# Down projection of a GEGLU feed-forward: seven block products for eight in the correction terms of seven of twelve pairs

## The chip, the cores and the metric

The kernel runs on one core of a Trainium2 chip. The metric is the device time of one execution in microseconds (us). Its engines are named as in the profile: PE (TensorE, matrix products), DVE (VectorE), ACT (ScalarE), POOL (GpSimd) and SP (which here only issues DMAs). Each engine works through its own list of instructions in order; semaphores hold an instruction back until what it needs from another engine is done.

## The reference

One transformer layer on 2048 tokens of width D = 640, in float32: attention with a sliding window of 256, then the feed-forward with F = 1536. Only the last matrix product is touched by the change.

```python
x = A_x
h = x + _A_ref(_layernorm(x, axis=-1), A_wqkv, A_wo)
h2 = h + _B_ref(_layernorm(h, axis=-1), B_w_gate, B_w_up, B_w_down)
# _B_ref(x, w_gate, w_up, w_down):
#   (_gelu(x @ w_gate) * (x @ w_up)) @ w_down
```

## The kernel before

**Numbers as pairs.** Float32 operands are split into a high and a low half in float16 (names ending in h and l). A float32 product is then three float16 products: high times high, and the two corrections high times low and low times high.

**Tiling of the feed-forward.** The tokens are cut into four chunks `c` of 512 (four blocks `b` of 128), the width F into three weight groups `fg` of 512 (four tiles `ft` of 128). `ORDER` lists the twelve pairs (c, fg): (0,0), (1,0), (0,1), (0,2), (1,1), (1,2), (2,0), (2,1), (2,2), (3,0), (3,1), (3,2). The first three are done by `gate_up`; the last nine by four calls of `quad` each, one for each `ft`, 36 quads in all, which I number 0 to 35. A quad makes gate and up projections with a scheme of seven block products for eight: its block results come to the PSUM tiles tp, ra, pv and rb (PE `MATMUL tp<-...` and so on), and `quad_out` combines them: ACT copies tp to SBUF, POOL adds the two halves, DVE runs eight operations (`rs<-pv`, two `gel<-ra`, `rs<-pv`, `rs<-rb`, `gel<-rs,ffk,gel`, `al<-gel,ah`; in the trace the tile rr or gelt is the SBUF copy of tp), ACT the gelu and the cast `ah<-gel`. The result is the activation of the pair as `ah` and `al`.

**The down projection.** `down(c, fg)` multiplies `ah`, `al` by the down weights of the group (`dh`, `dl`; in the trace w10h and w10l for group 0, w11 and w12 for groups 1 and 2). It makes eight output tiles (four blocks by two halves of 320 columns), each of 4 x 3 matmuls into a PSUM bank of the pool mm, which has two banks. `down_out` empties each bank with one DVE operation, `ht<-mm,ffk,ht`, which adds it to the float32 accumulator `ht` of the block. `down` of a pair does not run by itself: it is a generator, and `quad` calls `fill` at its end, which takes two tiles from it. So the eight tiles of a pair run in the four quads of the next pair, two after each quad, and only the last pair's `down` stands alone at the end.

**Who sets the order.** A planner (`Clock`, `Engine`, `Lane` and the loop at the end) runs at build time: it keeps a modelled time for each engine and lets the next operation of each generator be issued when its operands are modelled as ready. PE's own sequence in the feed-forward is fixed by the code (`dense_lane`); what DVE, ACT, POOL and SP do between is interleaved by the planner. Side lanes on DVE and POOL share the time of the quads: `norm_lane` and `token_sums` (normalise and pre-sum the next chunks, tiles wsl, ts, wst) and `weight_sums` (pre-sum gate and up weights, tile ws; kept in DRAM as `wsums` and loaded again by SP for pairs whose group has come up before).

Of the kernel before, what the change touches and what calls it, by code (L numbers as in the profile page):

```python
# [11 lines left out]
F32 = mybir.dt.float32  # L12
F16 = mybir.dt.float16
# [9 lines left out]
P = 128  # L23
NB = S // P
# [18 lines left out]
QE = -23  # L43
VE = -20
ME = 15
UE = -41
TE = 10


def _pow2(e):  # L50
    return float(2.0 ** e)
# [202 lines left out]
def block_kernel(ctx: ExitStack, tc: tile.TileContext, x, wqkv, wo, wg, wu, wd, out):  # L254
# [27 lines left out]
    def done(name):  # L282
        opened[name] -= 1
# [35 lines left out]
    def pe(*reads, slots=(), when=None):  # L319
        return ("tensor",), need(*reads, slots=slots, when=when)  # L320
# [23 lines left out]
    ones = const.tile([P, P], F32, name="ones")  # L344
    nc.vector.memset(ones, 1.0)


    NS = 16
# [114 lines left out]
    for g in range(FG):  # L463
        W["g", g] = Weight(wg[g], [KC, 512], C_G + g, GE)
        W["u", g] = Weight(wu[g], [KC, 512], C_U + g, GE)
        W["d", g] = Weight(wd[g], [FT, D], C_D + g)


    def layernorm(xt, lane, hi, lo, dst=None, when=None, xn=None, e=XE, tp="tp",
# [108 lines left out]
    def ff_scales_down(fg):  # L578
        ds_ = C_D + fg
        nc.vector.tensor_scalar(ffk[:, fg, 2:3], ffk[:, fg, 3:4], pw[:, ds_:ds_ + 1],  # L580
                                _pow2(-GE - XE - UE - GE - WE), op0=ALU.mult, op1=ALU.mult)


    wqp = ExitStack()
# [605 lines left out]
    def quad(c, fg, ft, fill):  # L1190
        fs = slice(ft * P, (ft + 1) * P)
        (gh, gl), (uh, ul) = (tuple(t[:, :, fs] for t in W[k, fg].hl) for k in "gu")
        hh, hl = hT[c]
        h1, h2 = hh[:, :, :CW], hh[:, :, CW:]
        l1, l2 = hl[:, :, :CW], hl[:, :, CW:]
        yield pe(slots=["tp"], when=lambda: c in TS and (c, fg, ft) in WS)
        t, s = TS[c], WS.pop((c, fg, ft))
        part = []
        tasks.append(quad_out(c, fg, ft, part))
        xs = bank("tp")  # L1200
        span(xs[:, CW:], gl, h1)
# [9 lines left out]
        span(gs[:, CW:], s[:, 3], l2, start=False)  # L1211
        yield pe(s[:, 2], t[:, 2], slots=["pv"])
        xs = bank("pv")
        span(xs[:, CW:], s[:, 2], t[:, 2])
        yield pe(s[:, 0], t[:, 0])
        span(xs[:, :CW], s[:, 0], t[:, 0])
        part.extend((xs, gs))
        yield pe(slots=["rb"])
        us = bank("rb")
        span(us, uh, hh, stop=False)  # L1220
        yield pe(t[:, 3])
        span(us[:, :CW], uh, t[:, 3], start=False)
        part.append(us)
        pos["quads"] += 1
        yield from fill()

    def quad_out(c, fg, ft, part):
        pool = ffpools[ORDER.index((c, fg)) % 2]
        ah, al = ga[c, fg]
        ra, rb = sums["r", ft % 2], sums["s"]  # L1230
        r2, r1 = ra[:, 0], ra[:, 1]
        r12, r21, r22 = (rb[:, k] for k in range(3))
# [12 lines left out]
        nc.vector.tensor_tensor(rb[:, :2], xs.rearrange("p (a n) -> p a n", a=2),  # L1245
                                r2.unsqueeze(1).to_broadcast([P, 2, CW]), op=ALU.add)
# [8 lines left out]
        nc.vector.tensor_tensor(r22, xs[:, :CW], r21, op=ALU.add)  # L1255
# [5 lines left out]
        nc.vector.tensor_tensor(flat(rb[:, 1:3]), part[3], flat(rb[:, 1:3]), op=ALU.add)  # L1261
        done("rb")
        yield on("vector", gel, rb)
        nc.vector.scalar_tensor_tensor(gel, flat(rb[:, 1:3]), ffk[:, fg, 1:2], gel, op0=ALU.mult,
                                       op1=ALU.mult)
        opened["s"] -= 1
        yield on("scalar", gel)
        nc.scalar.copy(ah[:, ft, :], gel)
        yield on("vector", ah[:, ft, :])
        nc.vector.tensor_tensor(al[:, ft, :], gel, ah[:, ft, :], op=ALU.subtract)  # L1270
        opened["gel"] -= 1
        pos["act", c, fg] += 1

    def down(c, fg):
        w = W["d", fg]
        yield pe(when=lambda: w.ready and w.down and pos["act", c, fg] == FT and c in hts)
        dh, dl = w.hl
        ah, al = ga.pop((c, fg))
        for b in range(CB):
            bs = slice(b * P, (b + 1) * P)  # L1280
            for nh in range(2):
                cs = slice(nh * 320, nh * 320 + 320)
                ps = yield from products(FT, lambda ft: parts((ah[:, ft, bs], al[:, ft, bs]),
                                                              (dh[:, ft, cs], dl[:, ft, cs])))
                tasks.append(down_out(c, fg, b, nh, ps))
                yield

    def down_out(c, fg, b, nh, ps):
        acc = hts[c][b]
        cs = slice(nh * 320, nh * 320 + 320)  # L1290
        yield on("vector", ps)
        nc.vector.scalar_tensor_tensor(acc[:, cs], ps, ffk[:, fg, 2:3], acc[:, cs], op0=ALU.mult,
                                       op1=ALU.add)
        done("mm")
        pos["down", c, b] += 1
        j = c * CB + b
        if pos["down", c, b] == 2 * FG:
# [3 lines left out]
        if j == NB - 1 and pos["down", c, b] > 2 * FG - 2:  # L1301
            nc.sync.dma_start(out[j * P:(j + 1) * P, cs], acc[:, cs])

    chunk = Counter()

    def load_h(c, pool, bufs):
        hts[c] = []
        for b in range(CB):
            j = c * CB + b
            ht = nc.tile(pool, [P, D], F32, "ht", bufs)  # L1310
            nc.sync.dma_start(ht, h_dram[j * P:(j + 1) * P, :])
            hts[c].append(ht)

    def chunk_lane(c):
        yield ("sync",), need(when=lambda: c == 0 or (ffpools[1] if c == 1 else
                                                      chunk["out", c - 2] == CB), eng="sync")
        load_h(c, ffpools[c % 2], CB)

    lnbuf = []

# [214 lines left out]
    def feed_forward():  # L1535
        quads = [(c, fg, ft) for c, fg in ORDER[PLAIN:] for ft in range(FT)]

        def sums_lane():
# [9 lines left out]
        sums["s"] = nc.tile(ffp, [P, 3, CW], F32, "rs")  # L1548
        prev = None
        for c, fg in ORDER[1:PLAIN]:  # L1550
            yield from gate_up(c, fg)
            if prev:
                yield from down(*prev)
            prev = (c, fg)
        for c, fg in ORDER[PLAIN:]:
            groups = down(*prev)

            def fill():
                for _ in range(2):
                    for y in groups:  # L1560
                        if y is None:
                            break
                        yield y

            pool = ffpools[ORDER.index((c, fg)) % 2]
            ga[c, fg] = tuple(nc.tile(pool, [P, FT, CB * P], F16, n) for n in ("ah", "al"))
            for ft in range(FT):
                yield from quad(c, fg, ft, fill)
            pos["gu", c] += 1
            prev = (c, fg)  # L1570
        yield from down(*prev)

    class Lane:
# [143 lines left out]
```

## Time and profile before

| what | value |
|---|---|
| time, median of three runs | 1014.95 us (1013.34 to 1016.89) |
| the profiled execution's own time | 1015.33 us |
| its span in the trace | 1013.6 us |
| PE / DVE / ACT / POOL busy | 98% / 74% / 44% / 31% of the span |
| the 36 quads | about 661 us to 994 us of the span, 9.24 us each |
| the last `down`, alone | 994 us to the end |

The trace gives, for each instruction, its start and length. Lengths of neighbouring instructions on one engine overlap by some tens of ns, since an instruction is begun before the one ahead of it has fully ended; what an instruction adds in a dense stretch is therefore the distance from its start to the next start. PE shows this most: matmuls follow each other much faster than one of them lasts.

### The profile page before, as it was taken

The numbers are of one execution on the slowest core, as the hardware profiler recorded it, in microseconds if no ns is written. First come the engines' busy times: TensorE is split into PE (matmuls) and PEld (weight loads), VectorE is DVE, ScalarE is ACT, GpSimd is POOL, SyncE is SP. The second block draws the span as 40 slices with busy tenths as digits, with TensorE's granted clock in tenths as the row PEclk, the third lists the DMA queues.
The fourth block names the chain that finished last, engine by engine and source line by source line (L and its number), as shares of the span: only waits on it lengthen the run. The fifth ranks groups of instructions, "written<-read, shape, count | busy, mean of one in ns | idle before, by whom it ended". The sixth has DMA issues, their size and how long they took to land.

```text
span 1013.6 us, 30516 instructions
## 1 busy us (share of the span) xinstructions
PE 996.3 (98%) x12798; PEld 696.4 (69%) x12798; DVE 754.7 (74%) x2212; ACT 442.5 (44%) x711; POOL 315.0 (31%) x504
## 2 busy tenths in 40 slices
PE   8999999999999999999999999999999999999998
PEld 7876777666666776776655654577777777777776
DVE  7888999786667877676688687798888875544553
ACT  5516666654555555554567634432222212221220
POOL 7004344643344333332345311254313300000000
PEclk9999999999999999999999999999999999999999
DMA  8658775291271714236004342323453542222211
GB/s 308 148 127 177 185 163 167 67 166 41 71 133 39 143 55 88 64 79 188 18 29 133 68 130 92 98 107 116 144 187 102 148 142 78 79 103 80 78 53 52
DMA packets 105834, 112.67 MB, mean 111 GB/s; under 512 B 38368, under 2 KB 79584, under 8 KB 105696
## 3 DMA queue, kind: packets, MB, share of 16 engines
q1 hardware_dynamic: 93600, 99.97, 36.7%
q10 hardware_dynamic: 12096, 10.75, 3.5%
q8 instruction: 100, 1.64, 0.7%
q14 instruction: 38, 0.31, 0.1%
HBM read 73.73 MB, written 28.84 MB: 101 GB/s over the span
## 4 chain that ended last, share of the span: by engine, by line
PE 86%; DVE 7%; DMA 3%; ACT 2%; issue 1%; SPq 1%; POOL 0%; ACTq 0%; DVEq 0%
PE mm L199 44%; PE pv L199 12%; PE ra L199 12%; PE rb L199 10%; PE tp L199 7%; DVE junk L199 1%; DMA kT<-qk 1%; SPq L199 1%; DVE am L199 1%; DMA wst<-in_wu_dram 1%; DMA qT<-in_wqkv_dram 1%; DMA wst<-in_wg_dram 1%; ACT pt L199 1%; DVE ht L199 0%; DVE w1l L199 0%
## 5 line engine op out<-in xcount | busy, mean ns | idle before, releaser
L199 POOL TENSOR_SCALAR_AFFINE_SELECT pt<-pt 128x512 f32<-128x512 f32 x352 | 174.8, 512 | 297.0 <-ACT pt L199 281.3
L199 DVE CUSTOM_DVE_ANT_0 junk<-rb,band 128x320 bf16<-128x320 f32 x228 | 111.5, 489 | 53.4 <-PE rb L199 48.8
L199 ACT ACTIVATE pt<-ra,esc 128x640 f32<-128x640 f32 (+2 forms) x132 | 100.6, 770 | 74.3 <-PE ra L199 69.3
L199 DVE CUSTOM_DVE_ANT_0 junk<-ra,band 128x320 bf16<-128x320 f32 x220 | 107.7, 489 | 33.2 <-PE ra L199 26.8
L199 ACT ACTIVATE pt<-rb,esc 128x640 f32<-128x640 f32 (+2 forms) x124 | 94.1, 764 | 82.4 <-PE rb L199 73.2
L199 PE MATMUL pv<-pt,v 128*21 128x128 f32 x2880 | 104.7, 279 | 0.0
L199 PEld LDWEIGHTS <-ah 128*128 128x128 f16 x768 | 75.1, 98 | 29.2 <-issue 1.9
L199 ACT ACTIVATE gel<-gel,ffk 128x512 f32<-128x512 f32 x36 | 26.0, 722 | 134.3 <-DVE gel L199 134.3
L199 PEld LDWEIGHTS pv<-pt,v 128*21 128x21 f32 x2880 | 70.0, 101 | 9.9 <-issue 1.0
L199 PEld LDWEIGHTS <-ws 128*128 128x128 f16 x720 | 70.5, 98 | 8.1
L199 PEld LDWEIGHTS <-qT 60*64 60x64 f16 x1280 | 29.8, 104 | 61.0 <-issue 51.9
L199 PEld LDWEIGHTS <-kT 62*64 62x64 f16 x2880 | 63.4, 107 | 11.2 <-issue 7.5
L199 PEld LDWEIGHTS <-gu 128*128 128x128 f16 x440 | 41.9, 98 | 36.1 <-issue 2.5
L199 DVE SCALAR_TENSOR_TENSOR ht<-mm,ffk,ht 128x320 f32<-128x320 f32 x96 | 52.1, 545 | 13.7 <-PE mm L199 11.8
L199 ACT CAST ah<-gel 128x512 f16<-128x512 f32 x48 | 29.6, 617 | 68.7 <-DVE gel L199 68.6
L199 PE MATMUL mm<-xh,w1h 128*128 128x256 f16 x200 | 54.6, 273 | 0.8 <-DVE qks L199 0.8
L199 PE MATMUL mm<-xl,w1h 128*128 128x256 f16 x200 | 54.7, 274 | 0.0
L199 PE MATMUL mm<-xh,w1l 128*128 128x256 f16 x200 | 54.6, 273 | 0.0
L199 POOL TENSOR_TENSOR gelt<-gelt 128x256 f32<-128x256 f32 x18 | 15.3, 852 | 112.0 <-ACT gelt L199 111.9
L199 PE MATMUL mm<-w3h,oh 128*128 128x320 f16 x160 | 48.3, 302 | 1.4 <-DVE qks L199 1.4
L199 PE MATMUL mm<-w3l,oh 128*128 128x320 f16 x160 | 48.2, 301 | 0.0
L199 PE MATMUL mm<-w3h,ol 128*128 128x320 f16 x160 | 48.1, 300 | 0.0
(313 smaller groups left out, 2562.6 us busy)
## 6 DMA issues: line engine op xcount, KB each, us to landing
ws<-wsums SPq DMA_DIRECT2D x24, 640.0 KB
qk<-qks ACTq DMA_DIRECT2D x32, 256.0 KB
qT<-qk SPq DMA_DIRECT2D x48, 160.0 KB
kT<-qk SPq DMA_DIRECT2D x48, 160.0 KB
wsums<-ws SPq DMA_DIRECT2D x12, 640.0 KB
ht<-in_x_dram SPq DMA_DIRECT2D x16, 320.0 KB
h_dram<-ht SPq DMA_DIRECT2D x16, 320.0 KB
ht<-h_dram SPq DMA_DIRECT2D x16, 320.0 KB
```

The lines of the kernel that those rows point to most:

```text
L199: r = real(*args, **kw)
```

## The change

For seven pairs, (1,1) to (3,1) (`SEVEN`), the correction products are arranged anew. Two token blocks b1, b2 and the two column halves 1, 2 form a two by two block product; of the high and low halves' products, four per pair of blocks are replaced by products of sums. For each pair of blocks `p` there are now eight PSUM tiles in four visits: a "z" tile of 4 matmuls, and a tile that goes to the accumulator with 8 or 4 (visits 1 and 3: 4 + 8; visit 2: 4 + 4; visit 4: 4 + 8). That is 44 matmuls in place of 48 for each `p`, and two `p` for each pair.

What is needed beside it: sums of the activations (`down7_sums`: two on DVE, tiles ts and sx, and two on POOL, for each `p`); sums of the weights (`down_sums_lane`: t2 and t4 on DVE and t3 on POOL, once for each group, kept in DRAM as `dsums` and loaded again by three DMAs when the group comes up again); a difference of the low weights in place (`diff_lane`, POOL, one for each group; that of group 2 is undone at the end by reloading `lows`, because the last pair uses the plain `down`); the four z tiles, kept in float32 SBUF tiles and added up over the groups of a chunk (ACT writes them for the first group of a chunk, DVE adds for the others: `to_z`); and `mix`, eight additions on DVE for each `p` at the end of a chunk's seven-product pairs, which carry the z tiles into the accumulators.

The order changes too: `quad` now calls `fill` in its middle, ahead of the products into pv, and again at its end, and each call takes one visit. The accumulators of chunks 2 and 3 now reuse those of the chunk before; the place of chunk 0's accumulators becomes the z tiles. Scales (`UE`, `GE`) change by powers of two, and an unused constant (`ones`) goes.

```diff
@@ quad
         yield pe(s[:, 3])
         span(gs[:, CW:], s[:, 3], l2, start=False)
+        yield from fill()
...
         yield pe(s[:, 2], t[:, 2], slots=["pv"])
         xs = bank("pv")
...
         part.append(us)
         pos["quads"] += 1
-        yield from fill()
@@ new
+    def down_sums_lane():
...
+        for g, (c, fg) in enumerate(SEVEN):
...
+            if fg in [f for _, f in SEVEN[:g]]:
+                for i, x in enumerate((t2, t3, t4)):
+                    yield ("sync",), lambda: nc.others(x, "sync") if free(min(7 + i, 8)) else INF
+                    nc.sync.dma_start(x.rearrange("p f n -> p (f n)"),
+                                      dsums[fg, :, i * FT * N2:(i + 1) * FT * N2])
...
+            else:
+                yield on("vector", d2, when=lambda: free(7) and pos["diff", fg])
+                nc.vector.scalar_tensor_tensor(t2, e2, _pow2(-TE), d2, op0=ALU.mult,
+                                               op1=ALU.subtract)
...
+                nc.gpsimd.tensor_tensor(t3, t2, d1, op=ALU.subtract)
...
+                nc.vector.scalar_tensor_tensor(t4, t2, -_pow2(TE), e1, op0=ALU.mult, op1=ALU.add)
...
+    def down7_sums(c, fg, p, g):
...
+        n = 8 * g + 4 * p
+        yield on("vector", ah, al, when=lambda: pos["visits"] >= n - 2)
+        nc.vector.scalar_tensor_tensor(s1, l2, _pow2(TE), h2, op0=ALU.mult, op1=ALU.add)
+        yield on("gpsimd", s1, ah, when=lambda: pos["visits"] >= n - 1)
+        nc.gpsimd.tensor_tensor(s2, s1, h1, op=ALU.subtract)
+        yield on("vector", s2)
+        nc.vector.scalar_tensor_tensor(s4, s2, -_pow2(-TE), l1, op0=ALU.mult, op1=ALU.add)
+        yield on("gpsimd", ah, when=lambda: pos["visits"] >= n)
+        nc.gpsimd.tensor_tensor(s3, h1, h2, op=ALU.subtract)
...
+    def down7(c, fg):
...
+                if fresh:
+                    nc.scalar.activation(z, ps, AF.Copy, scale=ffk[:, fg, 2:3])
+                else:
+                    nc.vector.scalar_tensor_tensor(z, ps, ffk[:, fg, 2:3], z, op0=ALU.mult,
+                                                   op1=ALU.add)
...
+            for first, second in (
+                    (([(h1, d1)], to_z(p, 0)), ([(h1, e1), (l1, e1)], to_acc(b1, 0))),
+                    (([(s1, d2)], to_z(p, 1), sums(0)), ([(h2, e2)], to_acc(b2, 1))),
+                    (([(s2, t2)], to_z(p, 2), sums(1)), ([(h1, e2), (s4, e2)], to_acc(b1, 1))),
+                    (([(s3, t3)], to_z(p, 3), sums(3)), ([(h2, e1), (l2, t4)], to_acc(b2, 0)))):
+                yield from tile7(*first)
+                yield from tile7(*second)
+                pos["visits"] += 1
+                yield
+            if (c, fg + 1) not in SEVEN:
+                tasks.append(mix(c, fg, p))
...
+    def mix(c, fg, p):
...
+        for o, i in ((a11, z1), (z6, z1), (a12, z5), (a12, z6), (z7, z6), (z5, z7), (a21, z7),
+                     (a22, z5)):
+            yield on("vector", o, i)
+            nc.vector.tensor_tensor(o, o, i, op=ALU.add)
```

How the instructions stand. First PE, in the middle of a quad of pair (1,2), between its products into ra and pv. Before, with nothing between:

```order
L199 LDWEIGHTS ws
L199 MATMUL ra<-h1l,ws 128x256
L199 LDWEIGHTS ws
L199 MATMUL pv<-ts,ws 128x256
L199 LDWEIGHTS ws
```

After, a visit begins there (sx holds one of the activation sums, ts_13754 the weight sums and the other activation sums):

```order
L199 LDWEIGHTS ws
L199 MATMUL ra<-h1l,ws 128x256
L199 LDWEIGHTS sx
L199 MATMUL mm<-ts_13754,sx 128x320
L199 LDWEIGHTS sx
```

The products into pv and rb, and all that DVE does with them, come one visit later in the quad than before.

Second DVE, where quad 9 (the second of pair (1,2)) begins its `quad_out`. Before:

```order
L199 TENSOR_TENSOR wst<-h0l,wst 128x256
L199 TENSOR_TENSOR rs<-pv,gelt 128x512
L199 TENSOR_TENSOR lyi<-lyi,lyai 128x1
L199 SCALAR_TENSOR_TENSOR wst<-h0l,h0h 128x256
L199 TENSOR_TENSOR gel<-ra,gelt 128x256
```

After:

```order
L199 SCALAR_TENSOR_TENSOR wst<-h0l,h0h 128x256
L199 SCALAR_TENSOR_TENSOR sx<-ts_13754,al 128x512
L199 TENSOR_TENSOR rs<-pv,gelt 128x512
L199 SCALAR_TENSOR_TENSOR ht<-mm,ffk,ht 128x320
L199 SCALAR_TENSOR_TENSOR ts_13754<-al,ah 128x512
L199 TENSOR_TENSOR gel<-ra,gelt 128x256
```

An activation sum that waits for POOL stands ahead of quad 9's first row now, and the emptying of an mm bank that visit 2 filled stands behind that row.

Third DVE, at the end of the program, from the last quad's `rs<-rb` on. Before:

```order
L199 TENSOR_TENSOR rs<-rb,rs 128x512
L199 SCALAR_TENSOR_TENSOR gel<-rs,ffk,gel 128x512
L199 SCALAR_TENSOR_TENSOR ht<-mm,ffk,ht 128x320
L199 TENSOR_TENSOR al<-gel,ah 128x512
L199 SCALAR_TENSOR_TENSOR ht<-mm,ffk,ht 128x320 x9
```

After:

```order
L199 TENSOR_TENSOR rs<-rb,rs 128x512
L199 SCALAR_TENSOR_TENSOR ht<-mm,ffk,ht 128x320
L199 SCALAR_TENSOR_TENSOR gel<-rs,ffk,gel 128x512
L199 SCALAR_TENSOR_TENSOR ht<-mm,ffk,ht 128x320 x2
L199 TENSOR_TENSOR ht<-ht 128x320 x2
L199 TENSOR_TENSOR al<-gel,ah 128x512
L199 TENSOR_TENSOR ht<-ht 128x320
L199 SCALAR_TENSOR_TENSOR ht<-mm,ffk,ht 128x320
L199 TENSOR_TENSOR ht<-ht 128x320 x2
L199 SCALAR_TENSOR_TENSOR ht<-mm,ffk,ht 128x320
L199 TENSOR_TENSOR ht<-ht 128x320 x3
L199 SCALAR_TENSOR_TENSOR ht<-mm,ffk,ht 128x320 x7
```

The last `mix` (the rows `ht<-ht`) stands among the rows that the plain `down` of the last pair waits for: `al<-gel,ah`, and the emptying of banks.

More of the change, by code (lines that the diff above doesn't have):

```diff
@@ L1304, in block_kernel, with chunk_lane @@
     chunk = Counter()
-    def load_h(c, pool, bufs):
+    def chunk_lane(c):
+        yield ("sync",), need(when=lambda: c == 0 or ffpools[1], eng="sync")
         hts[c] = []
         for b in range(CB):
+            yield ("sync",), lambda: (nc.slot(ffpools[min(c, 1)], "ht", CB)
+                                      if c < 2 or chunk["out", c - 1] > b else INF)
             j = c * CB + b
-            ht = nc.tile(pool, [P, D], F32, "ht", bufs)
+            ht = nc.tile(ffpools[min(c, 1)], [P, D], F32, "ht", CB)
@@ L1311, in load_h @@
             nc.sync.dma_start(ht, h_dram[j * P:(j + 1) * P, :])
             hts[c].append(ht)
[L1314 to L1317, printed above, removed]
+        if c == 1:
+            yield ("sync",), need(when=lambda: chunk["out", 0] == CB, eng="sync")
+            DS["z"] = [nc.tile(ffpools[0], [P, D], F32, "ht", CB) for _ in range(CB)]
@@ L1547, in feed_forward @@
             "p (a n) -> p a n", a=2)
-        sums["s"] = nc.tile(ffp, [P, 3, CW], F32, "rs")
+        sums["s"] = nc.tile(ffp, [P, 2, CW], F32, "rs")
         prev = None
@@ L1554, in feed_forward, with fill @@
             prev = (c, fg)
-        for c, fg in ORDER[PLAIN:]:
[L1556 to L1566, printed above, removed]
+        groups = deque()
+        def fill():
+            while groups:
+                for y in groups[0]:
+                    if y is None:
+                        return
+                    yield y
+                groups.popleft()
+        side.extend([(LATE, diff_lane()), (LATE, down_sums_lane())])
+        for c, fg in ORDER[PLAIN:]:
+            last, prev = prev, (c, fg)
             for ft in range(FT):
                 yield from quad(c, fg, ft, fill)
+                if ft == 0:
+                    groups.append((down7 if last in SEVEN else down)(*last))
+                yield from fill()
             pos["gu", c] += 1
-            prev = (c, fg)
+        while groups:
+            yield from fill()
         yield from down(*prev)
```

148 lines of the change are left out of this document (128 added, 20 removed).

## The prediction, made before the changed kernel was run

> **What bounds the kernel now.** I read the first lines of the page, then a table of busy time by stretches of the span.
>
> ```profile
> span 1013.6 us, 30516 instructions
> PE 996.3 (98%) x12798; PEld 696.4 (69%) x12798; DVE 754.7 (74%) x2212; ACT 442.5 (44%) x711; POOL 315.0 (31%) x504
> ```
>
> ```profile
> core 0: us, PE busy (x) PEld busy (x) DVE busy (x) ACT busy (x) POOL busy (x), PEclk, DMA share, GB/s
> 0.00:100.00 100.00, 95.13 (x999) 74.53 (x1000) 81.31 (x292) 49.56 (x98) 31.37 (x49) 1.00 0.71 190
> 100.00:200.00 100.00, 98.34 (x1636) 70.27 (x1636) 88.10 (x317) 65.42 (x108) 45.45 (x72) 1.00 0.60 149
> 200.00:300.00 100.00, 95.50 (x1903) 68.50 (x1906) 74.30 (x273) 54.41 (x86) 39.34 (x80) 0.97 0.53 105
> 661.20:809.10 147.90, 147.17 (x1098) 107.33 (x1097) 129.80 (x254) 38.71 (x60) 54.99 (x46) 1.00 0.42 129
> 809.10:994.00 184.90, 184.90 (x1383) 135.13 (x1381) 103.35 (x204) 38.56 (x61) 14.56 (x20) 1.00 0.26 87
> ```
>
> PE is the bound, and in the quads (661 to 994 us) it has hardly a gap at full clock (1.00). But DVE is second there, and unevenly: in the first sixteen quads it is busy 129.80 of 147.90 us (88%), in the last twenty 103.35 of 184.90 (56%). So fewer matmuls are time saved, as long as DVE and the engines behind it keep up, and the first sixteen quads are where that is in doubt.
>
> **What the removed matmuls are worth.** The chain that ended last shows one quad and its two plain tiles:
>
> ```profile
> 975.46 3.26 PE mm L199 x24
> ...
> 984.70 3.26 PE mm L199 x24
> ...
> 991.22 1.09 PE pv L199 x10
> 992.31 1.62 PE rb L199 x10
> 993.94 16.31 PE mm L199 x120
> ```
>
> 24 matmuls of 320 columns take 3.26 us: 0.136 us each (the length of a single one in the trace is more than twice that, since they overlap). A quad's period is 984.70 - 975.46 = 9.24 us. Each of seven pairs loses 8 of 96 matmuls: 56 x 0.136 = **7.6 us less PE work**, and the mean period where they run becomes 9.24 - 2 x 0.136 = 8.97 us.
>
> **What is added on DVE.** Prices, by groups of shape in the quads from 661 to 809 us, and for comparison two of them in the quiet ones from 846 to 994 us (second fence):
>
> ```profile
> L199 DVE SCALAR_TENSOR_TENSOR ht<-mm,ffk,ht 128x320 f32<-128x320 f32 x33 | 17.7, 540 | 1.0 <-PE mm L199 1.0
> L199 DVE TENSOR_TENSOR al<-gel,ah 128x512 f16<-128x512 f32 x15 | 14.6, 971 | 0.9 <-ACT ah L199 0.9
> L199 DVE SCALAR_TENSOR_TENSOR gel<-rs,ffk,gel 128x512 f32<-128x512 f32 x15 | 13.1, 876 | 0.0
> L199 DVE TENSOR_TENSOR rs<-rb,rs 128x512 f32<-128x512 f32 x15 | 10.2, 679 | 0.1
> L199 DVE TENSOR_TENSOR gel<-ra,gelt 128x256 f32<-128x256 f32 x7 | 2.9, 410 | 0.0
> L199 DVE SCALAR_TENSOR_TENSOR ws<-w9h,w9l 128x640 f16<-128x640 f16 x3 | 5.3, 1759 | 0.0
> L199 DVE SCALAR_TENSOR_TENSOR ws<-ws,gu 128x640 f16<-128x640 f16 x4 | 3.2, 812 | 0.0
> L199 DVE SCALAR_TENSOR_TENSOR wst<-h0l,h0h 128x256 f16<-128x256 f16 x5 | 2.0, 406 | 0.0
> ```
>
> ```profile
> L199 DVE SCALAR_TENSOR_TENSOR gel<-rs,ffk,gel 128x512 f32<-128x512 f32 x16 | 12.0, 751 | 1.7
> L199 DVE TENSOR_TENSOR al<-gel,ah 128x512 f16<-128x512 f32 x16 | 11.1, 692 | 3.6 <-ACT ah L199 3.6
> ```
>
> In a dense stretch a row costs about 0.08 us less than its length (below, `ht` starts at 765.95 and the next row at 766.41). So a z drain costs 0.46 us; an addition of `mix` (320 float32, between the 256 and the 512 of two rows above: 0.48) 0.40; an activation sum of 512 float16 (between 256 and 640: 0.68) 0.60; a weight sum of 1280 (twice 640, less the fixed part: 1.48) 1.40. POOL's new sums go by two of its rows, the first from the quads from 661 to 809 us, the second from those from 846 to 994:
>
> ```profile
> L199 POOL TENSOR_TENSOR ws<-gu 128x640 f16<-128x640 f16 x4 | 5.6, 1397 | 4.3 <-PE pv L199 2.4 <-issue 1.9
> L199 POOL TENSOR_TENSOR rr<-rr 128x256 f32<-128x256 f32 x8 | 5.8, 723 | 68.1 <-ACT rr L199 68.1
> ```
>
> On a line through them, 512 elements take 1.17 us, 1280 2.53.
>
> **Where it tips: ten quads.** In the new order of instructions, quads 8 to 17 (pairs (1,2) and (2,0), half of (2,1)) get the densest mix. Counted there: 8 z drains on DVE (3.7 us), 16 additions of `mix` (6.4), 12 activation sums (7.2), 4 weight sums (5.6): 22.9 us. The pre-sums of chunk 3 (20 rows `ts`, 5.3 us, by the `wst` row) and some of its normalisation (about 1.6) move out to later quads. POOL gets 12 sums of 512 (14.0 us), two of 1280 (5.1) and two in-place differences of 1280 (5.1): 24.2 us. Before, the same ten quads, from the `rs<-pv` of quad 8 to that of quad 18:
>
> ```profile
> 743.00:835.40 92.40, 92.40 (x692) 67.51 (x691) 78.62 (x174) 21.66 (x34) 23.05 (x22) 1.00 0.43 131
> ```
>
> DVE was busy 78.6 us, of which 3 are rows that stood alone and will overlap (some four in each quad, 0.08 each). So 78.6 - 3 + 22.9 - 6.9 = 91.6 us, and PE's ten quads are to take ten times 8.97 = 89.7. POOL doubles, to 47 us.
>
> **DVE and POOL get in each other's way.** Here DVE and POOL on the same stretch:
>
> ```profile
> 765.95 0.54 DVE L199 SCALAR_TENSOR_TENSOR ht<-mm,ffk,ht 128x320 f32<-128x320 f32 x1
> 766.41 1.64 DVE L199 SCALAR_TENSOR_TENSOR gel<-rs,ffk,gel 128x512 f32<-128x512 f32 x1
> 766.10 1.40 POOL L199 TENSOR_TENSOR ws<-gu,ws 128x640 f16<-128x640 f16 x1 [3.29 <-DVE ws L199]
> ```
>
> `gel<-rs,ffk,gel` takes 1.64 us where 0.75 is its quiet length, and it ends 0.55 after POOL's row; `ht<-mm`, which reads PSUM, is not stretched (540 ns here, as elsewhere). By groups: `al` is 0.28 us longer than in the quiet quads (x15: 4.2), `gel` 0.125 (x15: 1.9), `ws<-w9h` 0.95 longer than its neighbour of the same shape (x3: 2.8): 8.9 us in a stretch with 55.0 us of POOL, 0.16 us for each; with the tile wsl, not priced here, I put it at 0.2. After the change more of DVE's rows read two operands from SBUF (all of `mix` and the sums), so I take 0.27 for the ten quads: 47 x 0.27 - 23 x 0.2 = 8 us more. DVE's need is then 99.6 us against PE's 89.7, so 9.9 too much.
>
> [...]
>
> How much of the lag may DVE carry before PE waits? The emptying of mm banks bounds it: two banks, and a visit uses both. Before, DVE was already late without PE waiting: the `rs<-pv` of quads 11 and 12 start at
>
> ```profile
> 770.68 0.69 DVE L199 TENSOR_TENSOR rs<-pv,gelt 128x512 f32<-128x512 f32 x1 [1.24 <-PE pv L199]
> 781.95 0.68 DVE L199 TENSOR_TENSOR rs<-pv,rr 128x512 f32<-128x512 f32 x1
> ```
>
> 11.27 us apart where PE's period is 9.24, so some 2.0 us of lag cost nothing. That leaves 9.9 - 2.0 = 7.9 us; with 0.6 for DVE's rows that wait in line for a POOL sum (the row `sx` ahead of `rs<-pv` in quad 9), I take **8.5 us of PE waiting for emptied banks** in quads 8 to 18. Bounds: 0 if the contention adds nothing and lag is absorbed, 17 by the rival "worse".
>
> **The end.** The last quad of before, on DVE:
>
> ```profile
> 994.21 0.69 DVE L199 TENSOR_TENSOR rs<-rb,rs 128x512 f32<-128x512 f32 x1
> 995.00 0.75 DVE L199 SCALAR_TENSOR_TENSOR gel<-rs,ffk,gel 128x512 f32<-128x512 f32 x1
> 996.44 0.69 DVE L199 TENSOR_TENSOR al<-gel,ah 128x512 f16<-128x512 f32 x1 [0.22 <-ACT ah L199]
> ```
>
> PE's products into rb end at 993.94; two visits, again 24 matmuls, cover 3.26 us behind that. In the new order three drains and two additions of `mix` stand between `rs<-rb` and `al` (3 x 0.46 + 2 x 0.40 = 2.2 us, less the 0.7 that was spent on one drain and gaps), and one more addition and `al` ahead of the drain of visit 8's second bank. `al` then ends near 4.8 us behind rb, that drain near 5.7, and the second tile of the last `down`, due at 3.26 + 1.63 = 4.9 us, waits about **1.0 us** (0 to 2.5). The last drain itself stays last.
>
> **Priced at nothing.** Drains on ACT (24, none longer than about 0.7 us by the gelu-sized rows there) lie in ACT's 109 idle us of 661 to 809 and the like later. The new DMAs (three stores of 0.98 MB, twelve loads of 0.33) meet a DMA share of 0.43 or less, and the loads are asked for a quad and a half ahead; if one lands late, PE waits there, 0 to 3 us. Accumulators of chunks 2 and 3 load later, but the drain that needs them is two quads behind. Before the quads, the planner's order of the attention part shifts (a constant's memset is gone, 14 more warm-up products that nobody waits for): the work is the same and PE idles 11 us in the first 300, so it may gain or lose up to 2.5; I take 0.
>
> **The sum.** -7.6 + 8.5 + 1.0 = +1.9, and I add 0.6 for one late load: +2.5. The profiled execution took 1015.3 us (its span and 1.7 around it), 0.4 above the median of the three runs: 1015.3 - 0.4 + 2.5 = 1017.4, so **1017.5 us**.
>
> **Rivals.**
> - *The gain comes through* (25%): contention is no worse than before, and the lag of 91.6 against 89.7 is carried. Then -7.6 and 0 to 3 of waits: 1007.5 to 1011.5. For it: the quads before show no PE wait at 88% DVE. Against: 91.6 is already more than the time there is.
> - *Worse: POOL and DVE exclude each other* (22%): if half of POOL's 47 us holds DVE up (about half of DVE's time is then two-operand SBUF work), that is 23 us against the 4.6 now in it: 91.6 + 19 - 89.7 - 2 = 19 of waits, less 2 that lie behind each other: +17 - 7.6 + 1 = +10: 1022 to 1027. Its place is quads 8 to 17, the first mark `sx` and the drain behind it in quad 9. It decides from the point where DVE's need passes 99 us.
> - *The order of the attention part or the DMAs set the time* (5%): either sign.
> - *The change doesn't do what it says*: the order of instructions shows the 56 matmuls gone, so no chance is kept.
>
> **How the numbers follow.** A measurement of this kernel can tell about 0.3% (3 us) from no change. The forecast (48%) spans 1012 to 1021.5, of which 30% lie within 3 us of 1014.95 and 18% above. Faster by over 0.3%: 25 + 2 = 27%; within: 31%; slower: 18 + 22 + 2 = 42%. The range takes in the forecast, the upper part of the first rival and most of the second: 1008.5 to 1026.
>
> **What would show it.** PE's period in the quads: 8.97 us on the mean where DVE has room (quads 20 to 35) shows the first term; gaps of PE with `ht` on DVE as releaser, 8 us in all between quads 8 and 18 and the first in quad 9, the second; `gel`, `al` and `mix` rows longer than 0.8 us beside POOL rows, the contention; a gap of about 1 us in the last `down`, the third. No PE gaps in quads 8 to 18 would prove the DVE term wrong; gaps with a DMA as releaser, the zero for the loads.

## The result, and the profile after

| | before | after |
|---|---|---|
| time, median (us) | 1015.83 (4 runs) | 1039.70 (4 runs, 1038.66 to 1043.51) |
| ratio to before | | 1.0245, 95% interval 1.0212 to 1.0279 |
| span of the profiled execution (us) | 1013.6 | 1036.8 |

The changed kernel is slower by 2.45%, outside the predicted range. The head of its page:

```profile
span 1036.8 us, 30678 instructions
PE 994.8 (96%) x12756; PEld 692.3 (67%) x12756; DVE 835.7 (81%) x2325; ACT 452.1 (44%) x735; POOL 375.7 (36%) x538
```

DVE has 81 us more busy time than before, POOL 61. PE's busy time fell by 1.5 us only, though 56 products fewer should be worth 7.6. That is a weak hint that PE ran slower somewhere, since profiles with the same PE work differ by up to 3.6 us (992.7 to 996.3, the kernel before and two runs below). To find the place I took the start of PE's first product of each quad (the row into `tp` from `h` and a weight) from both timelines and subtracted:

| stretch | before | after | difference |
|---|---|---|---|
| start of the program to quad 0 | 663.27 | 667.40 | +4.1 |
| quads 0 to 7 | 75.07 | 76.08 | +1.0 |
| quads 8 to 18 | 101.63 | 121.26 | +19.6 |
| quads 19 to 34 | 147.83 | 144.54 | -3.3 |
| quad 35 and the end | 25.8 | 27.5 | +1.7 |

The sum is 23.1 of the 23.2 us between the spans. Without waits, quads 8 to 18 of the new order need 6 x 9.24 + 5 x 8.70 = 98.9 us (the two periods that stand undisturbed further on), so PE lost 121.26 - 98.9 = **22.3 us** there. The busy time of the engines in these eleven quads, before and after:

```profile
core 0: us, PE busy (x) PEld busy (x) DVE busy (x) ACT busy (x) POOL busy (x), PEclk, DMA share, GB/s
738.30:840.00 101.70, 101.70 (x762) 74.29 (x761) 85.03 (x185) 24.10 (x38) 23.78 (x23) 1.00 0.46 142
```

```profile
743.50:864.70 121.20, 103.63 (x741) 73.37 (x739) 116.11 (x201) 27.81 (x48) 53.79 (x39) 0.97 0.38 123
```

DVE got 16 instructions more (185 to 201) but 31 us more busy time, and now has 5 us left of the stretch. PE's granted clock is 0.97. What PE waited for in the same stretch of the changed kernel (us in total, times, longest):

```profile
PEld L199 <- issue: 18.2, 10, 5.6
PE mm L199 <- DVE ht L199: 16.2, 9, 5.4
```

The second row is the predicted one: products into `mm` wait until DVE has emptied a bank. (The first is the loading of the weights for the same products, held up beside them.) The longest, in quad 9, on PE's timeline (start, length, idle time before it and its releaser):

```profile
765.90 1.23 PE L199 MATMUL mm<-w11h,ah 128*128 128x320 f16 x4 [5.41 <-DVE ht L199]
766.92 1.27 PE L199 MATMUL mm<-w11h,sx 128*128 128x320 f16 x4
...
772.21 0.71 PE L199 MATMUL mm<-w11h,ah 128*128 128x320 f16 x4
772.75 0.71 PE L199 MATMUL mm<-ts,al 128*128 128x320 f16 x4
```

And what DVE and POOL of the changed kernel did ahead of it:

```profile
751.47 0.42 DVE L199 TENSOR_TENSOR rs<-pv,rs 128x256 f32<-128x256 f32 x1
751.82 2.45 DVE L199 SCALAR_TENSOR_TENSOR ts<-al,ah 128x512 f16<-128x512 f16 x1
754.19 0.68 DVE L199 TENSOR_TENSOR rs<-rb,rs 128x512 f32<-128x512 f32 x1
754.79 0.54 DVE L199 SCALAR_TENSOR_TENSOR ht<-mm,ffk,ht 128x320 f32<-128x320 f32 x1
755.25 2.04 DVE L199 SCALAR_TENSOR_TENSOR gel<-rs,ffk,gel 128x512 f32<-128x512 f32 x1
...
764.10 0.68 DVE L199 SCALAR_TENSOR_TENSOR sx<-ts,al 128x512 f16<-128x512 f16 x1
764.70 0.69 DVE L199 TENSOR_TENSOR rs<-pv,gelt 128x512 f32<-128x512 f32 x1
765.30 0.54 DVE L199 SCALAR_TENSOR_TENSOR ht<-mm,ffk,ht 128x320 f32<-128x320 f32 x1
```

```profile
751.11 2.61 POOL L199 TENSOR_TENSOR w12l<-w12l 128x1280 f16<-128x1280 f16 x1 [4.66 <-DMA lows<-w12l]
753.68 3.06 POOL L199 TENSOR_TENSOR w10l<-w10l 128x1280 f16<-128x1280 f16 x1
```

`ts<-al,ah`, quiet 0.68 us, takes 2.45 and ends half a microsecond after POOL's `w12l` row; `gel`, quiet 0.75, takes 2.04 and ends 0.55 after POOL's `w10l` row. The two rows between them that read PSUM (`rs<-rb` and `ht<-mm`) keep their lengths. `rs<-pv` of quad 9 starts 12.0 us after the quad's first product; in the run without POOL's reads (below) it starts after 7.5 us. So DVE is some 4.5 us late by then, and the drain that PE waits for stands where the order of instructions put it, behind `sx` and `rs<-pv` of quad 9.

The smaller differences: quad 6 is 1.5 us longer (below), quad 29 has one wait of 0.74 us on a drain (its period is 9.76 in place of 8.70), and otherwise quads 19 to 34 have the expected mean, (9.24 + 8.70) / 2 = 8.97 us. Of the +1.7 at the end 1.1 are no loss: as the filling work now starts half a quad later, one visit's 12 products (1.63 us) moved from quad 0 to behind quad 35, where another visit has 4 fewer; so 32 products stand between quad 35's start and the last `down` in place of 24. PE's wait in the end is one row, and with the product ahead of it, which starts 0.15 late, it costs 0.7 us from start to start:

```profile
1019.24 0.70 PE L199 MATMUL mm<-w11h,ah 128*128 128x320 f16 x4 [0.42 <-DVE ht L199]
```

### The profile page after: what moved, and what is told of

It reads as the page before. It is cut to its first block, busy times and chain, and to the rows that moved or that the text cites. A ratio compares the mean times of both kernels' runs of the same rounds, so it can differ in the third digit from the quotient of the medians.

```text
span 1036.8 us, 30678 instructions
## 1 busy us (share of the span) xinstructions
PE 994.8 (96%) x12756; PEld 692.3 (67%) x12756; DVE 835.7 (81%) x2325; ACT 452.1 (44%) x735; POOL 375.7 (36%) x538
## 4 chain that ended last, share of the span: by engine, by line
PE 70%; DVE 21%; DMA 4%; issue 3%; ACT 1%; POOL 0%; SPq 0%; DVEq 0%; ACTq 0%
PE mm L199 38%; PE pv L199 10%; PE ra L199 9%; PE rb L199 7%; PE tp L199 5%; DVE ht L199 3%; DVE junk L199 3%; DVE rs L199 2%; DVE gel L199 2%; DMA qk<-qks 2%; DMA kT<-qk 1%; DVE ts L199 1%; DVE wst L199 1%; DVE ws L199 1%; DVE al L199 1%
## 5 line engine op out<-in xcount | busy, mean ns | idle before, releaser
L199 DVE CUSTOM_DVE_ANT_0 junk<-rb,band 128x320 bf16<-128x320 f32 x222 | 108.6, 489 | 56.9 <-PE rb L199 51.6
L199 DVE CUSTOM_DVE_ANT_0 junk<-ra,band 128x320 bf16<-128x320 f32 x226 | 110.4, 489 | 33.0 <-PE ra L199 26.8
L199 ACT ACTIVATE pt<-ra,esc 128x640 f32<-128x640 f32 (+2 forms) x131 | 98.2, 757 | 77.1 <-PE ra L199 66.4
L199 ACT ACTIVATE pt<-rb,esc 128x640 f32<-128x640 f32 (+2 forms) x125 | 96.3, 775 | 65.6 <-PE rb L199 64.2
L199 DVE SCALAR_TENSOR_TENSOR ht<-mm,ffk,ht 128x320 f32<-128x320 f32 x128 | 68.4, 543 | 31.7 <-PE mm L199 31.7
L199 PEld LDWEIGHTS <-ah 128*128 128x128 f16 x600 | 58.8, 98 | 40.9 <-issue 19.7
L199 PE MATMUL mm<-xh,w0h 128*128 128x256 f16 x175 | 47.9, 274 | 0.0
```

The source lines that it names most:

```text
L199: r = real(*args, **kw)
```

## The experiments

The theories: **A**, GpSimd's new sums lengthen VectorE's rows with two SBUF inputs; **B**, VectorE has too many rows there at their quiet lengths; **C**, single late inputs or places in the order make the waits, not a sum of work; **D**, the 4.1 us ahead of the quads come from the planner alone. The runs without the tile of ones, with it charged again, without POOL's reads and without `mix` ran beside a median of 1016.26 us for the kernel before.

### The tile of ones alone, out and in

Out of the kernel before:

```
-    ones = const.tile([P, P], F32, name="ones")
-    nc.vector.memset(ones, 1.0)
```

> The kernel before with one edit: the 128 x 128 tile of ones and its memset, which nothing reads, are gone, as in the change. The planner's clock then stands 0.2 us earlier on VectorE from the start, and the order of the attention part comes out as it stands in the kernel after, instruction for instruction on TensorE up to the feed-forward part; the seven block products are not in. Theory D (the 4.1 us that the quads start later in the kernel after come from this shift of the plan alone): about 1020 us, 4 above the kernel before, and the first quad starts at about 667.4 us. Rival (the 4.1 us come from the change's own work or loads): within 1 us of the kernel before.

Measured: 1021.99 us, ratio 1.0069 (1.0042 to 1.0096). The first quad's first product, before, and without the memset:

```profile
663.27 0.71 PE L199 MATMUL tp<-h0h,w6l 128*128 128x256 f16 x5
```

```profile
668.27 0.71 PE L199 MATMUL tp<-h0h,w6l 128*128 128x256 f16 x5
```

Quad 0 is 1.15 us longer (11.54 for 10.39), since PE waits 1.8 us there for a weight's scale in place of 0.7; from quad 1 on the periods are those of before. Charged again in the kernel after:

```
+    nc.t["vector"] += nc.vector.cost("memset", ident, [])
```

> The kernel after with one edit: the planner's clock is charged on VectorE for a memset as long as that of the tile of ones (no instruction is added; the tile itself no longer fits), so that the order of the attention part is again that of the kernel before. Theory D: about 1035.5 us, 4 below the kernel after, first quad at about 663.3 us. Rival: 1039.7 us. Under both the waits of quads 9 to 18 stay at some 22 us, give or take 3 for a plan that comes out a little different there.

Measured: 1035.16 us, ratio 1.0193 (1.0160 to 1.0225), 4.5 us less than the kernel after (the two intervals overlap slightly). Quads 8 to 18 take 121.93 us, as expected no better. Theory D holds in both directions: removing a memset that nobody reads costs about 5 us, because it makes the planner lay out another order for the attention part. In one profile the start of quad 0 is a rough measure (665.83 us here, where 663.3 was expected), but the fourteen profiles of this case agree on the mean: the nine with the order of before start quad 0 at 659.2 to 666.8 us (mean 662.8), the five with the order of after at 665.2 to 669.4 (mean 667.8). About half of it lies in the first 100 us, where the two groups do not overlap: PE is busy for 93.9 to 95.4 us there in the nine and for 91.8 to 92.9 in the five. The longer wait in quad 0 belongs to the order too: it is in the kernel after, and not in this run (0.7 us). Which rows of the attention part are worse placed was not tried.

### GpSimd's reads taken away

```
+def _zero(nc, out, a, b):
+    nc.issue("gpsimd", nc.gpsimd.cost("tensor_tensor", out, [a, b]), [a, b], [out])
+    real = nc.gpsimd.real
+    real.tensor_tensor(out[:, :1, :8], a[:, :1, :8], b[:, :1, :8], op=ALU.subtract)
+    real.memset(out, 0.0)
...
-        nc.gpsimd.tensor_tensor(s2, s1, h1, op=ALU.subtract)
+        _zero(nc, s2, s1, h1)
```

and the same for s3, t3 and the weights' differences (`issue` charges the planner, so that the order stays; the sums' values are missing from the result).

> The kernel after with its order kept, but GpSimd's four kinds of new sums (s2, s3, t3 and the difference of the two column halves of the weights) are each replaced by a sum of 8 columns and a memset of the whole tile, which reads no SBUF; their values are left out of the result. VectorE's rows are all there. Theory A (GpSimd's new sums hold up VectorE's rows with two SBUF inputs, and that is most of the 22.3 us of waits in quads 9 to 18): the waits fall to some 5 to 8 us, the time to 1022 to 1027 us. Theory B (VectorE has too many rows there at their quiet lengths, and would be late without GpSimd): 1037 to 1040 us. Theory C (what counts is that GpSimd's differences come late, since they wait for a DMA that saves the columns first): quad 9's 6.6 us and little else stays or falls, 1033 to 1036 us.

Measured: 1023.26 us, ratio 1.0074 (1.0049 to 1.0099): theory A's range. Quads 8 to 18:

```profile
743.75:849.70 105.95, 99.94 (x742) 72.17 (x739) 101.07 (x203) 29.75 (x50) 40.86 (x55) 1.00 0.44 142
```

The waits fell from 22.3 to 105.95 - 98.9 = 7.0 us, DVE's busy time by 15.0, with all its rows in place; over the whole span it went from 835.7 to 812.1 us with the same 2325 instructions. Groups of DVE's rows over the whole span, of the kernel after (busy us, mean ns) and of this run:

```profile
L199 DVE SCALAR_TENSOR_TENSOR gel<-rs,ffk,gel 128x512 f32<-128x512 f32 x36 | 33.5, 930 | 0.3
L199 DVE TENSOR_TENSOR ht<-ht 128x320 f32<-128x320 f32 x48 | 24.9, 554 | 0.0
L199 DVE TENSOR_TENSOR rs<-rb,rs 128x512 f32<-128x512 f32 x36 | 24.7, 686 | 1.2
L199 DVE SCALAR_TENSOR_TENSOR sx<-ts,al 128x512 f16<-128x512 f16 x14 | 12.7, 907 | 0.0
```

```profile
L206 DVE SCALAR_TENSOR_TENSOR gel<-rs,ffk,gel 128x512 f32<-128x512 f32 x36 | 29.6, 823 | 0.3
L206 DVE TENSOR_TENSOR rs<-rb,rs 128x512 f32<-128x512 f32 x36 | 24.7, 686 | 1.2
L206 DVE TENSOR_TENSOR ht<-ht 128x320 f32<-128x320 f32 x48 | 21.5, 483 | 0.0
L206 DVE SCALAR_TENSOR_TENSOR sx<-ts,al 128x512 f16<-128x512 f16 x14 | 9.9, 706 | 0.0
```

The three kinds with two SBUF inputs got shorter; `rs<-rb`, with one input from PSUM, is 686 ns in both. Quad 6 took 9.63 in place of 10.74 us, so its delay, too, is mostly of this kind. But the memsets are also shorter than the sums (0.53 us for 1.2 to 1.3), so this run alone does not tell reading from being busy. The next pair does.

### The price by itself, on the kernel before

In quads 8 to 18, with the planner charged nothing for it (the scratch tile takes the place of the tile of ones, whose memset stays charged):

```
+        if 8 <= 4 * ORDER[PLAIN:].index((c, fg)) + ft < 19:
+            hh = hT[c][0]
+            for _ in range(2):
+                nc.gpsimd.real.tensor_tensor(ones.rearrange("p (a n) -> p a n", a=2),
+                                             hh[:, 0:2, :CW], hh[:, 2:4, :CW],
+                                             op=ALU.subtract)
```

> The kernel before, order kept, with two extra GpSimd subtractions of 128 x 512 fp16 out of SBUF in each of the quads 8 to 18 (22 in all, about 1.2 to 1.3 us each, 28 us), into a scratch tile that nothing reads; the scratch takes the place of the unused tile of ones, and the planner is charged as before. Nothing else of the change is in. Theory A (a reading GpSimd row lengthens VectorE's rows with two SBUF inputs by some 0.45 us per us, the 23.6 us by which VectorE's busy time fell over the 52 us of such rows in the run without them): VectorE, busy for 85.0 of 101.7 us there, comes to some 97 to 98 us, stays just under the period, and the time rises by 1 to 5 us through rows that come late singly; VectorE's busy time rises by 11 to 14 us. Theory B (only the number of VectorE's rows matters): no change of either.

and, as long but without reading, `nc.gpsimd.real.memset(ones, 0.0)` five times:

> As the run with the extra GpSimd subtractions in quads 8 to 18 of the kernel before, but with five memsets of the 128 x 512 scratch tile in place of each two subtractions (55 of 0.525 us, 29 us): GpSimd is busy as long, and reads nothing. Theory A: VectorE's busy time within 2 us of the kernel before and the time within 1.5 us of it. Rival (it is not the reading of SBUF but that GpSimd is busy, so that its own older sums come late): the same time as the run with subtractions.

Measured (before: 1016.70 us): 1020.62 us, ratio 1.0042 (1.0019 to 1.0066), with the subtractions; 1016.89 us, ratio 0.999 (0.9967 to 1.0014), with the memsets. The same quads in the one run and in the other:

```profile
735.40:841.80 106.40, 102.29 (x761) 74.00 (x759) 97.15 (x185) 23.67 (x38) 53.07 (x45) 1.00 0.44 135
```

```profile
734.20:835.90 101.70, 101.70 (x762) 74.30 (x760) 85.29 (x185) 24.09 (x38) 52.66 (x78) 1.00 0.46 141
```

POOL is busy for 53 us in both, DVE has 185 instructions in both and in the kernel before. With reads DVE needs 97.15 us, with writes alone 85.29, before 85.03. The 22 subtractions took 28.3 us, so each microsecond in which POOL reads costs DVE 12.1 / 28.3 = **0.43 us** in this mix; in the denser mix of the changed kernel, where the sums that read took 26.9 us of POOL in quads 8 to 18, the 15.0 us above make it 0.56. Theory A stands by itself: nothing of the change is in these kernels. POOL's 29.1 us of memsets cost DVE 0.3 us, its 28.3 us of subtractions 12.1. What grew with the reads are rows with two SBUF inputs, most of their kinds (`ts<-h1l,h1h` from 417 ns in the kernel before to 795, `wst<-h0l,h0h` from 406 to 595; with the memsets 415 and 406; but `ws<-ws,gu` 812 and 814); rows that read PSUM stayed (`ht<-mm` 543 and 539 ns, `rs<-rb` 680 and 677).

### DVE's rows taken away

```
-            nc.vector.tensor_tensor(o, o, i, op=ALU.add)
+            nc.issue("vector", nc.vector.cost("tensor_tensor", o, [o, i]), [o, i], [o])
```

The planner is charged, so that the order stays, and this part of the sum is missing from the result.

> The kernel after with its order kept, but the eight additions on VectorE that spread the four side sums over the accumulators after each pair of chunk and row pair are left out (64 rows of about 0.5 to 0.6 us; this part of the sum is missing from the result). 16 of them, 9.7 us, stand in quads 8 to 18. Theories A and B (VectorE is the bound over the whole stretch of quads 8 to 18, so that any of its time counts): waits fall by 7 to 10 us, the time to 1029 to 1033 us, with 1 us more at the end of the kernel where the last eight go. Theory C (single late inputs set the waits, not the sum of VectorE's work): 1036 to 1039 us.

Measured: 1033.78 us, ratio 1.0181 (1.0137 to 1.0225), 5.9 less than after; quads 8 to 18 take 115.35 us, waits 16.4. The stretch:

```profile
745.42:860.77 115.35, 103.99 (x742) 74.09 (x739) 106.94 (x186) 28.87 (x49) 52.92 (x39) 0.96 0.40 130
```

That lies between what the theories gave: DVE's work counts there, but 9.2 us of it taken away (116.11 to 106.94) give 5.9. The microsecond at the end did not come: quad 35 and the end take 27.5 us here too, so `mix` was not what lengthened them. Both edits together:

> The kernel after with its order kept, with both edits at once: GpSimd's four kinds of new sums are a few columns and a memset, and the eight additions that spread the side sums are left out (both parts are missing from the result). Without GpSimd's reads alone the stretch of quads 8 to 18 took 105.95 us, 7.0 above the 98.9 us that TensorE's work needs. Theory B for that rest (VectorE still has too many rows there: 101.1 us of 105.95 busy): 16 additions of 0.48 us are 7.7 us less, the waits fall to 0 to 3 us, the time to 1016 to 1020 us. Theory C for the rest (single late inputs): the rest stays, 1021 to 1024 us.

Measured: 1019.38 us beside 1014.83 for before, ratio 1.0055 (1.0030 to 1.0080). The time is in B's range, but quads 8 to 18 take 103.32 us: 4.4 of waits are left, which is again between B and C. The rest after theory A is a mixture: of its 7.0 us, 2.6 are the additions of `mix`, and 4.4 were not followed further.

### Fewer pairs

Five pairs in place of seven, with the planner charged for the ones:

```
-    SEVEN = ORDER[PLAIN + 1:-1]
+    SKIP = 2
+    SEVEN = ORDER[PLAIN + 1 + SKIP:-1]
```

(and the three conditions that count a chunk's pairs made to fit).

> The kernel after with the first two pairs, chunk 1 with groups 1 and 2, taken back to eight block products, so that five pairs (chunk 2 with all groups, chunk 3 with groups 0 and 1) have seven; and the planner is charged for the memset of the tile of ones, so that the attention part has its order of before. TensorE does 40 matmuls fewer than before (5.4 us) where the change does 56 fewer. The sums of the weights and the first tokens then stand in quads 12 to 18, when GpSimd and VectorE have few sums for gate and up left. Theory A: stalls of 0 to 4 us, 1010 to 1015 us, 0.2 to 0.6% below the kernel before. Rival (the new rows are too many in any quad): 1018 us or more.

Measured: 1017.33 us beside 1016.70 for before, ratio 1.0007 (0.9985 to 1.0030), in neither range. Quads 8 to 15 are free of waits now; by the periods 5.6 us stand in quads 17, 18, 20, 24 and 29, and eat the 5.4 that are saved. With `SKIP = 1`:

> As the version with five pairs, but with six (chunk 1 with group 2 too): 48 matmuls fewer than before (6.5 us). Its first sums stand in quads 9 to 15, beside the last sums of gate's and up's weights. Theory A: stalls of 5 to 14 us there, 1015 to 1024 us; theory C (what costs is the early start with one late difference in quad 8): 1010 to 1013 us.

Measured: 1027.50 us, ratio 1.0097 (1.0068 to 1.0125), beyond the upper end. Quads 8 to 18 take 115.46 us.

### The four sums on DVE

```
-        yield on("gpsimd", s1, ah, when=lambda: pos["visits"] >= n - 1)
-        nc.gpsimd.tensor_tensor(s2, s1, h1, op=ALU.subtract)
+        yield on("vector", s1, ah, when=lambda: pos["visits"] >= n - 1)
+        nc.vector.tensor_tensor(s2, s1, h1, op=ALU.subtract)
```

and so for s3, t3 and the differences. Five pairs (beside 1014.83 us for before):

> The version with five pairs (1017.3 us), with the same sums put on VectorE. Its waits are 5.6 us, in quads 17, 18, 20, 24 and 29, where VectorE is not short of time (109.4 of 137.6 us busy in quads 20 to 34) but single rows beside GpSimd's take 1.2 to 2.9 us. Rival C: without these the waits fall to 0 to 3 us, 1012 to 1015 us. Theory A with B: the rows that are added cost what the lengthening did, 1016 to 1018 us.

Measured: **1009.27 us**, ratio 0.9941 (0.9916 to 0.9966): faster than both kernels, and below either range. What PE waits for from 655 to 1010 us, first with five pairs and POOL's sums, then with the sums on DVE (in both, three waits on `ht`, 1.5 us together, stand ahead of quad 0 and behind quad 35's products into rb):

```profile
PE mm L199 <- DVE ht L199: 5.9, 10, 1.0
PE tp L199 <- DVE am L199: 0.7, 1, 0.7
```

```profile
PE mm L199 <- DVE ht L199: 1.5, 3, 0.7
```

From quad 1 to quad 34 every period is 9.24 or 8.70. DVE's busy time is the same in both, 813.0 and 812.7 us: the added rows cost what the lengthening did. My reading, not tested by itself, is that the planner places the added rows, while a row lengthened by POOL comes as a lump where no plan has room. With POOL's sums, ahead of one of these waits:

```profile
891.96 2.91 DVE L199 SCALAR_TENSOR_TENSOR ts<-ts,w12h 128x1280 f16<-128x1280 f16 x1 [1.81 <-PE mm L199]
894.79 0.54 DVE L199 SCALAR_TENSOR_TENSOR ht<-mm,ffk,ht 128x320 f32<-128x320 f32 x1
```

2.91 us in place of 1.48, and the drain stands behind it. Rival C wins in quads where DVE has time to spare. The same move with seven pairs, to be compared with 1035.16 us, the run with the same order of the attention part and POOL's sums:

> The kernel after with the plan's clock charged for the tile of ones (the attention part's order of before; 1035.2 us as it was), and with GpSimd's four kinds of new sums (s2, s3, t3, the weights' differences) put on VectorE. VectorE gets 28 rows of 128 x 512 fp16 and 6 of 128 x 1280 more, by the quiet rows of such operations (0.28 us for 256 columns, so some 0.55 and 1.4 us) 24 us in the whole kernel and some 14 in quads 8 to 18; by theory A it loses 23.6 us of lengthening, 15 of them there. Theory A with B (VectorE's whole work counts, however it comes about): busy time of VectorE and waits about as before the move, 1031 to 1037 us. Rival C (what costs is that GpSimd's rows lengthen VectorE's at places that the planner does not know of, so that drains fall behind them): waits fall by 8 to 14 us, 1021 to 1027 us.

Measured: 1034.99 us, ratio 1.0206 (1.0179 to 1.0233); here A with B was right. PE's two largest sums of waits from 655 to 870 us (0.4 of the second stand ahead of quad 0), and its quads 8 to 18:

```profile
PE tp L199 <- DVE wst L199: 12.7, 2, 8.7
PE mm L199 <- DVE ht L199: 5.2, 5, 2.6
```

```profile
733.26:859.28 126.02, 103.91 (x742) 73.63 (x740) 114.97 (x236) 30.58 (x51) 28.53 (x23) 0.93 0.40 127
```

POOL is back at 28.5 us, but DVE has 236 rows and is busy for 115 us of a stretch in which PE needs 98.9. The waits moved: now the token sums of chunk 2 (`wst`) come last, and quad 12, their first reader, takes 24.2 us. With six pairs on DVE:

> Six pairs with seven block products (chunk 1 with group 2 too), the four sums on VectorE. TensorE does 48 matmuls fewer than before (6.5 us; the version with five pairs on VectorE: 5.4 us, no waits, 1009.3 us). Theory A with B (in quads 12 to 15 VectorE's whole work counts: 42.9 us busy of 43.5 there in the run with six pairs and GpSimd's sums, 35.2 of 37.0 in the run with five pairs on VectorE): the sums of one more pair and the first weight sums, which now stand beside the token sums of chunk 2, leave 4 to 10 us of waits in quads 9 to 18, 1012 to 1019 us. Rival C (only unplanned lengthening makes waits): none, 1007 to 1010 us.

Measured: 1026.28 us beside 1017.39 for before, ratio 1.0078 (1.0054 to 1.0101); a miss for both theories. Quads 8 to 11 run without waits at 32.90 us of DVE in 36.95, and then quad 12 alone takes 24.20:

```profile
PE tp L199 <- DVE wst L199: 11.1, 4, 5.7
```

DVE had 4 us to spare ahead of that, 2.6 of them in quad 8, which points to the order, with the token sums placed too late, as with seven pairs. This is not shown: whether another order would make six pairs pay was not tried.

## Why the prediction was wrong

The mechanism, its place and its first mark were as forecast; its size was not, and a term put at nothing was not nothing. By the prediction's steps:

- **-7.6 for 56 products: right.** Quads 19 to 34 show the mean period of 8.97 us, but for the 0.74 us wait in quad 29; five pairs without waits in the quads gained 5.6 us where 5.4 of products are saved.
- **+8.5 for waits on emptied banks: this step failed by its size; it was 22.3.** The first wait was in quad 9, on the drain behind `sx` and `rs<-pv`, as said. The step was the sum 9.9 - 2.0 + 0.6. (a) The price of the contention was too low. It was put at 0.27 us for each of POOL's, from the averages of rows before the change, which gave 8; the run without POOL's reads shows 15.0 in quads 8 to 18, and the run on the kernel before 0.43 for each added. So the averages of before were too low a measure. It may be that much of POOL's time there ran beside rows that read PSUM; this was not measured. (b) The count of rows was about right: without POOL's reads DVE grew by 101.07 - 85.03 = 16.0 us over eleven quads, where the prediction has 13.0 for ten. Together DVE needs 116.1 us against PE's 98.9: 17.2 too much, not 9.9. Of that difference of 7.3 us, 7.0 are the contention. (c) For lag that costs nothing and rows that wait in line the prediction took -2.0 + 0.6 = -1.4. In their place stand +5.1, the time in which DVE was idle in the stretch (121.2 - 116.1) while PE was late too, 6.5 more than that; how they divide between the two was not followed.
- **0 for the order of the attention part: wrong**, +4.1 in the profile, 4.5 to 5.7 in the medians of the two runs that changed this alone. It was bounded at 2.5 because PE idles only 11 us in the first 300 us; but another order may also add idle time, and did (14.5 us there in the changed kernel).
- **+0.6 for a late load: none came.** The sums that the changed kernel loads back were never what PE waited for. A DMA was late elsewhere: POOL's difference of `w12l` waited 4.66 us for the saving of the columns, and then ran beside DVE's dense rows at the end of quad 8. That it came late seems to have done little by itself: with the same delay but no reads (the run without them) quad 9 is 1.1 us too long, not 6.6.
- **+1.0 at the end: 0.7**; the other 1.1 us are the 8 products more there. Its cause was not as forecast: leaving `mix` out did not shorten the end.
- Not in the sum: quads 0 to 7. Quad 6 lost 1.5 us, mostly to GpSimd's reads (0.4 without them), and quad 0 lost 1.15, in which PE waited 1.8 us for a weight's scale, 0.7 before; that comes from the order of the attention part, as the two runs on it show.

These terms close: -7.6 for the products, +22.3 in quads 8 to 18, +4.1 and +1.15 for the order of the attention part, +1.5 in quad 6, +1.1 in quad 29 and +0.7 at the end are 23.2 us, the difference of the spans.

The rival "worse" had the right engines, place and first mark, but only 17 us of waits, and nothing for the order of the attention part or for quads 0 to 7. That POOL and DVE exclude each other, so that half of POOL's time holds DVE up, was the author's assumption and is shown by no run; what the runs showed is 0.43 and 0.56 us of DVE for each microsecond in which POOL reads, and 0.3 us for 29.1 us of memsets.

## What to carry to other kernels

When work goes to an idle GpSimd, price what it does to VectorE: in this kernel each microsecond of a reading GpSimd row cost VectorE 0.43 to 0.56 us, paid by its rows with two SBUF inputs, and a plan that does not know of it has its drains late even where VectorE has time (5.6 us of waits with five pairs). If the same sum costs VectorE as much as the lengthening would, try it there, where the order can see it; here that paid with five pairs (1009.27 us), and not with six or seven, where VectorE was short of time (seven) or, as it seems, its rows stood in a worse order (six). Price the contention by putting dummy reads into the kernel before, not by averages over rows that may not have met POOL's; and when a change touches the input of a planner, even by a dead constant, compare the untouched part of the program by itself.

## What the runs showed of the hardware

Behind some of PE's waits stood slow products. After the 5.41 us wait in quad 9, four products of 320 columns took 1.23 to 1.27 us where they take 0.71 five microseconds later, and the granted clock of quads 8 to 18 was 0.97; PE was busy for 103.63 us there, and for 99.94, at a granted clock of 1.00, with the same work when the waits were short (the run without POOL's reads). So about 3.7 us of the 22.3 are PE's own slower work, though in a stretch that DVE bounds it can't be said that all of them add to the time. In the timelines of quads 8 to 18 of the changed kernel and of the run with seven pairs on DVE, the products behind waits of up to 1.94 us had their usual lengths. Slow ones stood behind 2.60 us (seven pairs on DVE: 1.00 and 1.27 us for four products of 320 columns), 3.03 us (the changed kernel: 1.22 and 1.27) and 5.41 us, and behind 8.66 and 4.01 us close together (seven pairs on DVE: 2.34 us for five products of 512 columns, quietly 1.24); behind 3.18 us, in the run with seven pairs on DVE, there were none (1.24). So in these two runs the length of the wait alone does not tell which products are slow.
